# A pair's second 64-row passes on 64 rows of TensorE, two side by side

## The chip, the cores and the metric

The kernel runs on one core of a Trainium2 chip. Times are device microseconds (us) of one execution. The time of the kernel before is the median of three runs. The profile is of one further execution, and every duration below that is not called a run's time is from it. The engines are named as in the profile: PE is TensorE (matmuls), PEld its weight loads, DVE is VectorE, ACT is ScalarE, POOL is GpSimd, SP issues transfers.

## What is computed

One pre-normalised transformer layer on 2048 tokens of width 576, all in 32-bit floats: an attention half (32 heads of 18, each query seeing 8 keys at distances 0, 2, ..., 14), then a gated feed-forward half of width 4608. The change touches only the feed-forward half.

```python
def _B_ref(x, w_gate, w_up, w_down):
    g = jnp.einsum("bsd,df->bsf", x, w_gate)
    u = jnp.einsum("bsd,df->bsf", x, w_up)
    h = _sigmoid(g) * u
    return jnp.einsum("bsf,fd->bsd", h, w_down)

h = x + _A_ref(_layernorm(x, axis=-1), A_wqkv, A_wo)
h2 = h + _B_ref(_layernorm(h, axis=-1), B_w_gate, B_w_up, B_w_down)
```

## The kernel before

**Precision.** A matmul here reads its operands in a shorter float format. To keep 32-bit accuracy every operand is split into a high half and a low half (`split`, L103 to L106: ACT copies to the short format, DVE subtracts to get the rest), and a product is three matmuls: high x high, high x low, low x high. `prod` (L557) does that for two 128-row slices of the inner dimension, so it is six matmuls of 128 rows by 512 tokens.

**The 64-row rest.** The inner dimension is 576 = 4 x 128 + 64. The last 64 rows are held twice, in rows 0 to 63 and again in rows 64 to 127 of one slice. For the activations `split_rest` (L108) puts the high half into all 128 rows and then overwrites rows 64 to 127 with the low half. For the weights both copies are split alike, into a high tile (index 0) and a low tile (index 1). `rest` (L566) then needs two matmuls over 128 rows: with the high weights (a = 0) it gives high x high and high x low at once, and with the low weights (a = 1) it gives low x high, plus low x low.

**Chunks.** The 4608 columns of the feed-forward are worked off in chunks of 128 (NF = 36), for four blocks of 512 tokens, in two halves p = 0 and p = 1. `items` lists them in order: 14 chunks of kind "std" for p = 0 (one block, function `single`), 22 of kind "pair" for p = 0 (two blocks at once), 14 std and then 36 pair for p = 1: 58 pair chunks in all. A pair chunk computes gate and up of two blocks by seven products instead of eight (a scheme of sums and differences of sub-matrices: a00, a01, a11 and s1 to s4 are activations or their sums, t1 to t4 and b00, b10, b11 weights or their sums), and four rests: gate ("g4") and up ("u4") for each of the two blocks.

**A pair chunk** (`pair`, L623) has three accumulators in PSUM, one bank each: b1, b2, b3. Their contents are taken off on the way into s1, s2, s3 in SBUF by ACT copies and DVE additions (L628, L633, L638, L645, L646, L651), and sigmoid is applied to s1 and s2 (L634, L652). `last` multiplies: s1 by what b1 holds at the end, s2 by s3 (L582, or L985 where the results are kept for a seven-product down projection). `between(i)` puts other work between the products: the down projection of earlier chunks (L671 for ordinary ones, L733 for the seven-product kind that the second 36 pair chunks use), and in the first 22 pair chunks attention and output projection of the two later blocks. In those, `between(6)` and `between(4)` issue two units of it, in the last 36 each `between` issues one. A unit of `down_seven` is six matmuls of 288 columns, a unit of the ordinary kind twelve.

**Order.** The program text is not the final order: a scheduler places the instructions of each engine by priorities (`tc.high_priority`) and by the engines' expected load. Every engine then works through its own list strictly in order, and waits at semaphores. A bank is written again only when what it held has been read: the next chunk's first product into b1 waits for DVE's multiplication of s1 by b1, and the product "t4" into b3 waits for the DVE addition of L646.

Of the kernel before, what the change touches and what calls it, by code (L numbers as in the profile page):

```python
# [17 lines left out]
AF = mybir.ActivationFunctionType  # L18
ALU = mybir.AluOpType
# [34 lines left out]
HC = 700  # L54
# [7 lines left out]
def kernel(ctx, tc, x, wqkv, wo, wmlp, out):  # L62
    nc = tc.nc
    dve, act, pool, pe, sp = nc.vector, nc.scalar, nc.gpsimd, nc.tensor, nc.sync
# [34 lines left out]
    def f32(ap):  # L99
        return ap.bitcast(F32)  # L100
# [3 lines left out]
    def split(hi, lo, src):  # L104
        act.activation(hi, src, AF.Copy)  # L105
        splits.append(dve.tensor_tensor(lo, src, f32(hi), ALU.subtract))  # L106

    def split_rest(t, src):  # L108
        act.activation(t, src, AF.Copy)
        dve.tensor_tensor(t[64:128], src[64:128], f32(t[64:128]), ALU.subtract)  # L110

    def pads(g):
        for e in range(2):
# [162 lines left out]
    def th_tile():  # L276
        return xt.tile([P, 5, TB], F32R, tag="th", bufs=3, name="th")

    def tl_tile():
        return xt.tile([P, 4, TB], F32R, tag="tl", bufs=4, name="tl")  # L280

    def x_half(raw, rest):
        t = tl_tile() if rest is None else th_tile()
        split(t[:, 0:2], t[:, 2:4], raw)
        if rest is not None:
            split_rest(t[:, 4], rest)
        return t


    xt = ctx.enter_context(sb_pool("xt"))  # L290
# [53 lines left out]
    def qkv_w(g):  # L344
        w = saw.tile([P, 2, 5, NQ], F32R, tag="qw", bufs=2, name="qw")
        if g == 0:
            wr = swo.tile([P, 5, NQ], F32, tag="wo", name="wr")
        for c in range(5):
            ws = wr[:, c] if g == 0 else sas.tile([P, NQ], F32, tag="wst", bufs=3, name="ws")
            sp.dma_start(ws, wqkv[g][:, c * NQ:(c + 1) * NQ])  # L350
            with tc.high_priority(3 * HI if g == 0 else HI):
                split(w[:, 0, c], w[:, 1, c], ws)
        return w
# [59 lines left out]
    w = [qkv_w(0)]  # L413
# [63 lines left out]
    X = {}  # L477
# [79 lines left out]
    def prod(ps, xx, w, n, first):  # L557
        wt, k0 = w[n]
        k = 0
        for c in range(2):  # L560
            for a, m in ((0, 0), (0, 2), (1, 0)):
                pe.matmul(ps, wt[:, a, k0 + c], xx[:, m + c], start=first and k == 0,  # L562
                          stop=k == 5, skip_group_check=True)
                k += 1

    def rest(ps, xx, w, n):  # L566
        wt, k0 = w[n]
        for a in range(2):
            pe.matmul(ps, wt[:, a, k0], xx[:, 4], start=False, stop=a == 1,  # L569
                      skip_group_check=True)  # L570

    gc_bufs = 3

    def halves(name, src):
# [10 lines left out]
    def s_tile():  # L585
        return gh.tile([P, TB], F32, tag="s", bufs=4, name="s")

    def b_tile(i):
        return gp.tile([P, TB], F32, name=f"b{i % 3 + 1}")
# [31 lines left out]
    added = [None]  # L621

    def pair(X, w, between, last):  # L623
        b1, b2, b3 = b_tile(0), b_tile(1), b_tile(2)
        s1, s2, s3 = s_tile(), s_tile(), s_tile()
        prod(b1, X["a00"], w, "b00", True)
        with tc.high_priority(HC):
            act.activation(s1, b1, AF.Copy)  # L628
        between(0)
        prod(b2, X["a01"], w, "b10", True)  # L630
        rest(b2, X["a01"], w, "g4")
        with tc.high_priority(HC):
            added[0] = dve.tensor_tensor(s1, s1, b2, ALU.add)  # L633
            act.activation(s1, s1, AF.Sigmoid)  # L634
        between(1)
        prod(b1, X["s2"], w, "t2", False)
        with tc.high_priority(HC):
            act.activation(s2, b1, AF.Copy)  # L638
        between(2)
        prod(b3, X["s3"], w, "t3", True)  # L640
        between(3)
        prod(b1, X["s1"], w, "t1", False)
        rest(b1, X["a11"], w, "u4")
        with tc.high_priority(HC):
            act.activation(s3, b1, AF.Copy)  # L645
            added[0] = dve.tensor_tensor(s3, s3, b3, ALU.add)  # L646
        between(4)
        prod(b3, X["a11"], w, "t4", False)
        rest(b3, X["a11"], w, "g4")
        with tc.high_priority(HC):  # L650
            added[0] = dve.tensor_tensor(s2, s2, b3, ALU.add)  # L651
            act.activation(s2, s2, AF.Sigmoid)  # L652
        between(5)
        prod(b1, X["s4"], w, "b11", False)
        rest(b1, X["s4"], w, "u4")
        with tc.high_priority(HC):
            last((s1, b1), (s2, s3))
        between(6)

# [158 lines left out]
    def operands(pp, p, Xn, names, a0, a1):  # L818
        if p == 0:
            a0 = pp.tile([P, 5, TB], F32, name="ar0")  # L820
            pool.dma_start(a0, xscr[0])
        s = [pp.tile([P, 2, TB], F32, name=f"rs{i}") for i in range(3)]
        rd = pp.tile([P, TB], F32, name="rd")
        if p == 1:
            for n in ("a00", "a01"):
                a = a0[:, 0:2] if n == "a00" else a0[:, 2:4]
                with tc.high_priority(HI):
                    Xn[n] = x_half(a, None if n == "a00" else a0[:, 4])
                yield
        raw = yield from sums(a0, a1, a1[:, 0:2] if p == 1 else a0[:, 0:2], *s, rd)  # L830
        for n in names:
            with tc.high_priority(HI):
                Xn[n] = x_half(*raw[n])
            yield
        return raw

# [13 lines left out]
    Xn = {}  # L850
# [33 lines left out]
    raw = None  # L884
# [165 lines left out]
    for c, (kind, p, f) in enumerate(items):  # L1050
        w, d = wc
        for b, late_c in ((0, NF + NSTD - 3), (1, NF + NSTD + 5)):
            if c == late_c:
                e, hf = BLOCKS[b]
                pool.dma_start(ov[e, hf], hacc[b])
        skip = () if kind == "std" else (3,)
        by_seven = c >= NF + NSTD
        if c == NSTD:
            finish_bg()
            last_x = splits[-1]  # L1060
            bg = under_rest(getattr(last_x, "ins", last_x))
        if c == NF + NSTD:
            finish_bg()
            with tc.high_priority(HI):
                for n in ("s1", "a11"):
                    Xn[n] = x_half(*raw[n])
            X = Xn
            pp_stk.close()
            dw = ctx.enter_context(sb_pool("dw", "right"))
        if c + 1 < len(items):  # L1070
            wc = weights(items[c + 1][0], wg, c + 1 < NF + NSTD)
        if c + 2 < len(items):
            wg = load_gu(items[c + 2][2], n=WC if c + 2 < NF + NSTD else GU)
        hid = {}
        blocks = [p] if kind == "std" else [2 * p, 2 * p + 1]

        def last(h0, h1):
            hid[0] = hidden(*h0, "h0")
            hid[1] = hidden(*h1, "h1")

        if kind == "std":
            hid = single(X, w, p, late, twice)
        elif not by_seven:
            side = last_pair if c == NF - 1 else bg_step

            def between(i):
                if i in (4, 6):
                    units(2)
                side(i)

            pair(X, w, between, last)
        else:
            def between(i):
                nonlocal st, gc, gc_bufs, dk
                units(1)
                if c == NF + NSTD and i == 5:
                    assert not queue
                    st_stk.close()
                    gc_stk.close()
                    gc = gc_stk.enter_context(sb_pool("gc2"))  # L1100
                    st = st_stk.enter_context(sb_pool("st2"))
                    dk = dk_stk.enter_context(sb_pool("dk", "right"))
                    for n in ("s4h", "s4l", "s1h"):
                        dk.tile([P, TB], F32R, name=n)
                    gc_bufs = 2
                down_side(f, i)

            pair(X, w, between, last if f >= NF - NPL else last_sums(f))
            if f < NF - NPL:
                if f % 2:  # L1110
                    if f == 1:
                        queue.append(lag(LAG))
                    queue.append(seven())
                continue
            d = M[f]
        seg.append((hid, d))
        if len(seg) == 2:
            if by_seven and f == NF - NPL + 1:
                queue.append(load_tails())
            for b in blocks:  # L1120
                queue.append(down_std(seg, b, f // 2) if kind == "std" else
                             down_tail(seg, b, f == NF - 1) if by_seven else down_units(seg, b))
            seg = []
# [44 lines left out]
```

## Time and profile before

| | |
|---|---|
| time, median of 3 runs | 1635.3 us (1633.71 to 1636.6) |
| span of the profiled execution, first to last instruction | 1628.5 us, 6.8 us under the median of the runs |
| mean granted TensorE clock | 0.987 |
| first pair chunks (22), us from the span's start | about 410 to 799 |
| last pair chunks (36), then the rest of the down projection | 988 to about 1600, to 1628.5 |
| ACT busy | 888.6 us (55%) |
| matmuls in all / in second passes of rests | 8532 / 288 of 576 under L569 |

A busy matmul in the profile includes the time until its last result is out, so that two in a row overlap; the distance of their starts tells the speed. Idle time of PE shorter than that overlap doesn't show as idle.

### The profile page before, as it was taken

How to read it: one execution, taken by the hardware profiler on the slowest of the kernel's cores; microseconds unless marked ns; L12 is line 12 of the kernel's file. 1: busy time of each engine (PE TensorE's matmuls, PEld its weight loads, DVE VectorE, ACT ScalarE, POOL GpSimd, SP SyncE). 2: the span in 40 equal slices, each digit the busy share in tenths (PEclk: the TensorE clock that was granted, in tenths of full speed). 3: DMA queues.
4: the chain of work that ended last, by engine and by line, in shares of the span. 5: the costliest groups of instructions: out<-in, count | busy, mean ns of one | idle time of the engine just before them, and what ended most of it. 6: DMA issues, size and time to landing. Idle time of an engine off the chain costs nothing.

```text
span 1628.5 us, 22454 instructions
## 1 busy us (share of the span) xinstructions
PE 1573.4 (97%) x8532; PEld 1387.9 (85%) x8532; DVE 1265.6 (78%) x1982; ACT 888.6 (55%) x1565; POOL 188.9 (12%) x230
## 2 busy tenths in 40 slices
PE   6799999989999999999989999999999999999998
PEld 6699988778888888888878988888888888888888
DVE  6899898847999999999636677777667777667755
ACT  5423235425556556655534344777667777667761
POOL 2000010010000100100101100112222121211210
PEclk9999999989999999999999999999999999999999
DMA  6545745565665666576685224698888888888883
GB/s 214 184 141 187 264 179 189 156 194 158 194 160 152 168 151 169 160 184 161 171 249 181 100 87 132 141 186 169 177 173 164 184 180 166 181 170 170 189 174 121
DMA packets 77789, 278.23 MB, mean 171 GB/s; under 512 B 8336, under 2 KB 14224, under 8 KB 76784
## 3 DMA queue, kind: packets, MB, share of 16 engines
q0 software_dynamic: 28944, 111.19, 36.1%
q1 hardware_dynamic: 40304, 143.70, 26.7%
q10 hardware_dynamic: 8432, 21.89, 3.5%
q8 instruction: 67, 1.10, 0.3%
q14 instruction: 42, 0.34, 0.1%
HBM read 145.88 MB, written 133.23 MB: 171 GB/s over the span
## 4 chain that ended last, share of the span: by engine, by line
PE 77%; DVE 10%; DMA 8%; issue 2%; ACT 2%; SPq 0%; POOL 0%; ACTq 0%; DVEq 0%; POOLq 0%
PE b L562 39%; PE dp L671 13%; PE dp L733 11%; PE b L569 7%; DMA wg<-in_wmlp_dram 3%; PE acc L151 3%; DVE pr L173 2%; DVE pr L199 2%; DVE lg L176 1%; DMA o<-kw 1%; PE bgp L151 1%; PE b L151 1%; DVE w L106 1%; DMA oj<-o 1%; DMA kw<-k 1%
## 5 line engine op out<-in xcount | busy, mean ns | idle before, releaser
L562 PE MATMUL b<-tl,w 128*128 128x512 f32 x1728 | 446.4, 397 | 3.0 <-ACT w L105 2.1
L562 PEld LDWEIGHTS b<-tl,w 128*128 128x128 f32 x1728 | 313.0, 189 | 64.5 <-ACT w L105 2.9
L562 PE MATMUL b<-th,w 128*128 128x512 f32 x1380 | 362.0, 397 | 4.4 <-DVE s L646 4.3
L562 PEld LDWEIGHTS b<-th,w 128*128 128x128 f32 x1380 | 252.1, 189 | 59.2 <-DVE s L646 9.7
L569 PE MATMUL b<-th,w 128*128 128x512 f32 x576 | 178.1, 390 | 0.0
L105 ACT ACTIVATE w<-wg 128x384 fp32r<-128x384 f32 (+2 forms) x200 | 117.4, 595 | 111.1 <-DMA wg<-in_wmlp_dram 60.1
L106 DVE TENSOR_TENSOR w<-wg,w 128x384 fp32r<-128x384 f32 (+2 forms) x200 | 128.4, 648 | 63.0 <-ACT w L105 59.5
L739 ACT ACTIVATE ev<-dp 128x576 f32<-128x576 f32 x224 | 145.1, 648 | 33.5 <-PE dp L733 30.7
L742 POOL DMA_DIRECT2D h<-ev x128 | 110.6, 864 | 454.7 <-ACT ev L739 438.0
L151 PE MATMUL acc<-qw,th 128*128 128x432 f32 x512 | 156.8, 368 | 4.3 <-ACT th L105 4.3
L106 DVE TENSOR_TENSOR w<-tw,w 128x512 fp32r<-128x512 f32 x116 | 79.6, 687 | 72.2 <-ACT w L105 71.3
L569 PEld LDWEIGHTS b<-th,w 128*128 128x128 f32 x576 | 108.4, 188 | 23.3
L671 PE MATMUL dp<-d,h1h 128*128 128x288 f32 x640 | 120.5, 297 | 6.5 <-ACT stage L679 6.5
L671 PE MATMUL dp<-d,h0h 128*128 128x288 f32 x640 | 119.2, 296 | 3.0 <-ACT h0h L105 2.1
L105 ACT ACTIVATE w<-tw 128x512 fp32r<-128x512 f32 x116 | 73.2, 631 | 89.4 <-PE b L562 84.1
L671 PEld LDWEIGHTS dp<-d,h1h 128*128 128x128 f32 x640 | 99.4, 190 | 9.7 <-ACT stage L679 6.7
L151 PEld LDWEIGHTS acc<-qw,th 128*128 128x128 f32 x512 | 99.5, 194 | 9.5 <-ACT th L105 4.8
L671 PEld LDWEIGHTS dp<-d,h0h 128*128 128x128 f32 x640 | 99.4, 189 | 7.0 <-ACT h0h L105 2.3
L679 ACT ACTIVATE stage<-dp 128x576 f32<-128x576 f32 x112 | 72.0, 645 | 53.9 <-PE dp L671 42.6
L151 PE MATMUL acc<-qw,tl 128*128 128x432 f32 x256 | 94.4, 369 | 0.0
L362 ACT ACTIVATE ev<-acc 128x432 f32<-128x432 f32 x64 | 33.9, 532 | 106.7 <-PE acc L154 96.2
L173 DVE TENSOR_TENSOR pr<-kw,q 128x1152 f32<-128x1152 f32 x64 | 85.0, 1352 | 7.6 <-DMA kw<-k 7.0
(268 smaller groups left out, 2892.7 us busy)
## 6 DMA issues: line engine op xcount, KB each, us to landing
h<-ev POOLq DMA_DIRECT2D x96, 576.0 KB, 6.8
wg<-in_wmlp_dram SPq DMA_DIRECT2D x49, 928.0 KB, 4.9
h<-stage POOLq DMA_DIRECT2D x28, 1152.0 KB, 10.8
wg<-in_wmlp_dram SPq DMA_DIRECT2D x36, 640.0 KB, 4.8
kw<-k SPq DMA_DIRECT2D x16, 792.0 KB, 4.8
vw<-v SPq DMA_DIRECT2D x16, 792.0 KB, 5.5
wd<-in_wmlp_dram SPq DMA_DIRECT2D x18, 576.0 KB, 6.7
h<-ev POOLq DMA_DIRECT2D x32, 288.0 KB, 6.1
```

Source lines behind the costliest of these rows:

```text
L105: act.activation(hi, src, AF.Copy)
L106: splits.append(dve.tensor_tensor(lo, src, f32(hi), ALU.subtract))
L151: pe.matmul(ps[:, :n], a[:, c, js], m[:, c], start=k == 0, stop=False)
L173: dve.tensor_tensor(pr[:, i], kw[:, j:j + W], q[:, j].unsqueeze(1).broadcast_to([P, W, CG]), ALU.mult)
L362: act.activation(ev[:, :, j], ps[:, :NQ].rearrange("p (t c) -> p t c", t=3), AF.Copy)
L562: pe.matmul(ps, wt[:, a, k0 + c], xx[:, m + c], start=first and k == 0, stop=k == 5, skip_group_check=True)
L569: pe.matmul(ps, wt[:, a, k0], xx[:, 4], start=False, stop=a == 1, skip_group_check=True)
L671: pe.matmul(ps[:, i, :DH2], a[:, js], d[:, m, i * DH2:(i + 1) * DH2], start=k == 0, stop=k == n)
L679: act.activation(hv, ps, AF.Copy)
L733: pe.matmul(ps[:, i, :DH2], a[x][:, js], m[y], start=k in (0, 1, 3) and q == 0, stop=q == 2, skip_group_check=True)
L739: act.activation(hs[:, k % 2], ps[:, :, :DH2], AF.Copy)
L742: pool.dma_start(hsev[:, u, k0:k + 1], hs[:, :k + 1 - k0], accum_op=ALU.add, max_dma_last_dim=8 * D)
```

## The change

`rest` stays for std chunks. In a pair chunk it is taken apart. `rest_full` does the pass with the high weights over 128 rows, where the rest was before. The pass with the low weights needs only the 64 rows in which the activation's high half lies; `rest_halves` issues two such passes, of two different rests into two different banks, one in rows 0 to 63 (UP) and one in rows 64 to 127 (DOWN). So that each couple has one of both, the operand a11 now holds its low half in rows 0 to 63 and its high half in rows 64 to 127 (`low_of`), the other way round than a01 and s4. Low x low falls away.

The first couple (b2 with a01 and g4, b1 with a11 and u4) stands behind the product t3, ahead of t1. The second (b3 with a11 and g4, b1 with s4 and u4) stands at the chunk's end. With them DVE's addition and ACT's sigmoid of s1 move behind the first couple, and those of s2 to the chunk's end, ahead of `last`.

```diff
-    def split_rest(t, src):
+    def split_rest(t, src, low=slice(64, 128)):
         act.activation(t, src, AF.Copy)
-        dve.tensor_tensor(t[64:128], src[64:128], f32(t[64:128]), ALU.subtract)
+        dve.tensor_tensor(t[low], src[low], f32(t[low]), ALU.subtract)
...
+    UP, DOWN = slice(0, 64), slice(64, 128)
+
+    def low_of(name):
+        return UP if name == "a11" else DOWN
...
+    def rest_full(ps, xx, w, n):
+        wt, k0 = w[n]
+        pe.matmul(ps, wt[:, 0, k0], xx[:, 4], start=False, stop=True, skip_group_check=True)
+
+    def rest_halves(*outs):
+        for (ps, xx, n, rows), w in outs:
+            wt, k0 = w[n]
+            pe.matmul(ps, wt[rows, 1, k0], xx[rows, 4], start=False, stop=True,
+                      skip_group_check=True)
...
         prod(b2, X["a01"], w, "b10", True)
-        rest(b2, X["a01"], w, "g4")
-        with tc.high_priority(HC):
-            added[0] = dve.tensor_tensor(s1, s1, b2, ALU.add)
-            act.activation(s1, s1, AF.Sigmoid)
+        rest_full(b2, X["a01"], w, "g4")
...
         prod(b3, X["s3"], w, "t3", True)
         between(3)
+        rest_halves(((b2, X["a01"], "g4", UP), w), ((b1, X["a11"], "u4", DOWN), w))
+        with tc.high_priority(HC):
+            added[0] = dve.tensor_tensor(s1, s1, b2, ALU.add)
+            act.activation(s1, s1, AF.Sigmoid)
         prod(b1, X["s1"], w, "t1", False)
-        rest(b1, X["a11"], w, "u4")
+        rest_full(b1, X["a11"], w, "u4")
...
         prod(b3, X["a11"], w, "t4", False)
-        rest(b3, X["a11"], w, "g4")
+        rest_full(b3, X["a11"], w, "g4")
+        between(5)
+        prod(b1, X["s4"], w, "b11", False)
+        rest_full(b1, X["s4"], w, "u4")
+        rest_halves(((b3, X["a11"], "g4", DOWN), w), ((b1, X["s4"], "u4", UP), w))
         with tc.high_priority(HC):
             added[0] = dve.tensor_tensor(s2, s2, b3, ALU.add)
             act.activation(s2, s2, AF.Sigmoid)
-        between(5)
-        prod(b1, X["s4"], w, "b11", False)
-        rest(b1, X["s4"], w, "u4")
-        with tc.high_priority(HC):
             last((s1, b1), (s2, s3))
         between(6)
```

Where the operands are made, `x_half(*raw[n])` becomes `x_half(*raw[n], low_of(n))`.

The order that the scheduler makes of it, at three places of one of the last 36 pair chunks. First PE from the product t3 to the rest of "u4" (b1 to b3 are the accumulators, th and tl activations, w1 to w4 weights, dp an accumulator of the down projection, h0h and h0l its operands). Before:

```order
L562 MATMUL b3_11860<-tl_8823,w2_11651 128x512 x6
L733 MATMUL dp_11919<-d_11691,h0h_11632 128x288
L733 MATMUL dp_11919<-d_11691,h0l_11633 128x288
L733 MATMUL dp_11919<-d_11691,h0h_11632 128x288 x2
L733 MATMUL dp_11919<-d_11691,h0l_11633 128x288
L733 MATMUL dp_11919<-d_11691,h0h_11632 128x288
L562 MATMUL b1_11858<-tl_9155,w3_11652 128x512 x6
L569 MATMUL b1_11858<-th_9158,w4_11650 128x512 x2
```

The same place after the change:

```order
L567 MATMUL b3_11860<-tl_8823,w2_11651 128x512 x6
L749 MATMUL dp_11916<-d_11691,h0h_11632 128x288
L749 MATMUL dp_11916<-d_11691,h0l_11633 128x288
L749 MATMUL dp_11916<-d_11691,h0h_11632 128x288 x2
L749 MATMUL dp_11916<-d_11691,h0l_11633 128x288
L749 MATMUL dp_11916<-d_11691,h0h_11632 128x288
L584 MATMUL b2_11859<-th_8744,w1_11647 128x512
L584 MATMUL b1_11858<-th_9158,w4_11650 128x512
L567 MATMUL b1_11858<-tl_9155,w3_11652 128x512 x6
L579 MATMUL b1_11858<-th_9158,w4_11650 128x512
```

The two rows of L584 are the couple, of 64 rows each (the sizes printed are those of the result); one row of the rest behind t1 is gone. The couple's second half is the first in this chunk to need the low half of the weights w4, and it waits for both DVE and ACT, the wait for one of them being an instruction of its own in PE's queue.

Second, PE at the chunk's end, up to the next chunk's first product into b1. Before:

```order
L562 MATMUL b1_11858<-th_8826,w4_11650 128x512 x5
L569 MATMUL b1_11858<-th_8826,w4_11650 128x512 x2
L733 MATMUL dp_11981<-d_11766,s3h_11823 128x288
L733 MATMUL dp_11981<-d_11766,s3l_11824 128x288
L733 MATMUL dp_11981<-d_11766,s3h_11823 128x288 x2
L733 MATMUL dp_11981<-d_11766,s3l_11824 128x288
L733 MATMUL dp_11981<-d_11766,s3h_11823 128x288
L733 MATMUL dp_11919<-d_11812,s1h_11827 128x288
L733 MATMUL dp_11919<-d_11812,s1l_11828 128x288
L733 MATMUL dp_11919<-d_11812,s1h_11827 128x288 x2
L562 MATMUL b1_12008<-tl_8727,w1_11840 128x512 x6
```

And after the change, from the couple at the chunk's end on:

```order
L584 MATMUL b3_11860<-th_9158,w1_11647 128x512
L584 MATMUL b1_11858<-th_8826,w4_11650 128x512
L749 MATMUL dp_11981<-d_11766,s3h_11823 128x288
L749 MATMUL dp_11981<-d_11766,s3l_11824 128x288
L749 MATMUL dp_11981<-d_11766,s3h_11823 128x288 x2
L749 MATMUL dp_11981<-d_11766,s3l_11824 128x288
L749 MATMUL dp_11981<-d_11766,s3h_11823 128x288
L749 MATMUL dp_11916<-d_11812,s1h_11827 128x288
L749 MATMUL dp_11916<-d_11812,s1l_11828 128x288
L749 MATMUL dp_11916<-d_11812,s1h_11827 128x288 x2
L749 MATMUL dp_11916<-d_11812,s1l_11828 128x288
L749 MATMUL dp_11916<-d_11812,s1h_11827 128x288
```

Behind these stand one matmul of the next chunk's "b10" into b2 and then its first product into b1. Between the old chunk's last matmul and the next one into b1 there were 10 matmuls of 288 columns; now there are 12 and one of 512.

Third, DVE at the same chunk's end (s, r00 and r10 are gate, up and their products; tw and w are the weights of later chunks). Before:

```order
L651 TENSOR_TENSOR s_11862<-s_11862,b3_11860 128x512
L106 TENSOR_TENSOR w3_11845<-tw_11846,w3_11845 128x512
L106 TENSOR_TENSOR w1_11990<-wg_11856,w1_11990 128x640
L985 TENSOR_TENSOR r00_11973<-s_11861,b1_11858 128x512
L985 TENSOR_TENSOR r10_11979<-s_11862,s_11863 128x512
L106 TENSOR_TENSOR w4_11843<-wg_11663,w4_11843 128x384
```

After:

```order
L106 TENSOR_TENSOR w3_11845<-tw_11846,w3_11845 128x512
L548 TENSOR_TENSOR tw_11996<-wg_11856 128x512
L549 TENSOR_TENSOR tw_11996<-wg_11856,tw_11996 128x256
L671 TENSOR_TENSOR s_11862<-s_11862,b3_11860 128x512
L1001 TENSOR_TENSOR r00_11973<-s_11861,b1_11858 128x512
L106 TENSOR_TENSOR w4_11843<-wg_11663,w4_11843 128x384
```

The addition of b3 to s2 (L671, L651 before) now stands right ahead of the multiplication that frees b1 (L1001, L985 before), and both wait for the couple; the weight splits that stood between them have moved ahead or behind.

More of the change, by code (lines that the diff above doesn't have):

```diff
@@ L280, in tl_tile, with x_half @@
         return xt.tile([P, 4, TB], F32R, tag="tl", bufs=4, name="tl")
-    def x_half(raw, rest):
+    def x_half(raw, rest, low=slice(64, 128)):
         t = tl_tile() if rest is None else th_tile()
@@ L285, in x_half @@
         if rest is not None:
-            split_rest(t[:, 4], rest)
+            split_rest(t[:, 4], rest, low)
         return t
+    UP, DOWN = slice(0, 64), slice(64, 128)
+    def low_of(name):
+        return UP if name == "a11" else DOWN
     xt = ctx.enter_context(sb_pool("xt"))
@@ L832, in operands @@
             with tc.high_priority(HI):
-                Xn[n] = x_half(*raw[n])
+                Xn[n] = x_half(*raw[n], low_of(n))
             yield
@@ L1065 @@
                 for n in ("s1", "a11"):
-                    Xn[n] = x_half(*raw[n])
+                    Xn[n] = x_half(*raw[n], low_of(n))
             X = Xn
```

## The prediction

> **What bounds the kernel now.** I read the page's engine totals first, then the chain that ended last, then busy time by stage, then PE's rows in order of time.
>
> ```profile
> PE 1573.4 (97%) x8532; PEld 1387.9 (85%) x8532; DVE 1265.6 (78%) x1982; ACT 888.6 (55%) x1565; POOL 188.9 (12%) x230
> PE 77%; DVE 10%; DMA 8%; issue 2%; ACT 2%; SPq 0%; POOL 0%; ACTq 0%; DVEq 0%; POOLq 0%
> PE b L562 39%; PE dp L671 13%; PE dp L733 11%; PE b L569 7%; DMA wg<-in_wmlp_dram 3%; PE acc L151 3%; DVE pr L173 2%; DVE pr L199 2%; DVE lg L176 1%; DMA o<-kw 1%; PE bgp L151 1%; PE b L151 1%; DVE w L106 1%; DMA oj<-o 1%; DMA kw<-k 1%
> ...
> L569 PE MATMUL b<-th,w 128*128 128x512 f32 x576 | 178.1, 390 | 0.0
> ```
>
> PE is busy 97% of the span and 77% of the chain runs through it; the rests (L569) alone are 7% of the chain. DVE and DMA have their share of the chain mostly in the attention, ahead of the pair chunks. In the stages where the change acts:
>
> ```profile
> 410.00:799.00 389.00, 385.65 (x2108) 339.25 (x2107) 371.31 (x502) 224.97 (x368) 29.96 (x28) 1.00 0.63 165
> 988.00:1628.50 640.50, 634.39 (x3386) 548.27 (x3384) 454.62 (x770) 422.65 (x736) 112.55 (x130) 1.00 0.81 169
> ```
>
> The columns are length, then busy time of PE, PEld, DVE, ACT and POOL, granted clock, DMA share, GB/s. The first row is the 22 pair chunks of p = 0: PE is idle 3.4 us of 389, so a matmul saved there is time saved, but DVE is busy 371.3 of 389 (95%) as well. The second is the 36 pair chunks of p = 1 and the tail: PE idle 6.1 us of 640.5, DVE 71%. The granted clock is 1.00 in both, so there is no clock to win or lose at the level seen.
>
> **What a rest costs.** Duration is not the price, since matmuls overlap. In order of time:
>
> ```profile
> 701.09 0.62 PE L569 MATMUL b<-th,w 128*128 128x512 f32 x2
> 701.54 1.52 PE L562 MATMUL b<-th,w 128*128 128x512 f32 x6
> 702.90 0.62 PE L569 MATMUL b<-th,w 128*128 128x512 f32 x2
> 703.36 0.42 PE L671 MATMUL dp<-d,h0h 128*128 128x288 f32 x2
> ```
>
> Six matmuls start within 702.90 - 701.54 = 1.36 us, 0.227 us each, and a rest's two take 0.46 us. One lasts 0.390 us (the L569 row), so the last 0.163 us of each lie beneath the next one.
>
> **Removed:** four second passes in each of 58 chunks, 4 x 58 x 0.227 = 52.7 us of PE. **Added:** two couples of 64-row matmuls in each chunk, 116 couples. No row of this trace has a matmul over fewer than 128 rows, so a couple's price is bounded. From below: both stream at once and it takes one place, 0.227 us; saving 116 x 0.227 = 26.3 us. From above, without a cost at its borders: the halves follow each other, 0.454 us; saving nothing. Between them stands how far ahead a second weight load can go.
>
> ```profile
> 700.87 0.41 PEld L569 LDWEIGHTS b<-th,w 128*128 128x128 f32 x2
> 701.32 0.41 PEld L562 LDWEIGHTS b<-th,w 128*128 128x128 f32 x2
> 79.23 0.66 PE L140 MATMUL mm<-ident,tok 128*128 128x128 f32 x4 [1.52 <-ACT tok L132]
> ```
>
> The first two rows begin one matmul ahead: the rest's loads begin at 700.87 while its matmuls begin at 701.09, and the loads of the next product at 701.32, 0.23 after 701.09, with the rest's second matmul. One load is made ahead, and the next begins when that matmul has begun. The third row shows what a load needs where matmuls are too short to hide it: four transposes of 128 columns in 0.66 us, each lasting 0.273 in the median of its group, so (0.66 - 0.273) / 3 = 0.129 us from start to start with a load for each.
>
> ```profile
> L140 PE MATMUL mm<-ident,tok x80: 270/273/476, 9.1 to 221.8; 128*128 128x128 f32 x80
> ```
>
> If the second half's load begins only with the first half's matmul, the second half starts 0.129 us behind the first, and the couple takes 0.227 + 0.129 = 0.356 us. I take this value, since every load in the rows behaves so; it saves 0.454 - 0.356 = 0.098 us per couple, 116 x 0.098 = **11.4 us** (4.3 in the first stage, 7.1 in the second).
>
> The Trainium skill, "TensorE: Matmul & The Clock Gate", section "Part 3: Packing small matmuls — row/col tiling", says that matmuls in different row groups start about 4 ns apart and that a load overlaps a running matmul when its row group differs. By it a couple would be an estimated 0.231 us and the saving 25.9 us; no run here shows it yet, and its bound is in the range already.
>
> **What moves, and its cover.** (1) The addition and sigmoid of s1 go behind the first couple. s1 is needed by `last` at the chunk's end, some 7 us of PE work later: nothing. (2) The couple needs the copy of b1 to s2 done; t1, which stood at that place, needed the same: nothing. The low half of w4 is needed eight matmuls earlier (1.8 us), but it is split near the chunk's start:
>
> ```profile
> 1381.34 1.64 PE L562 MATMUL b<-tl,w 128*128 128x512 f32 x6
> ...
> 1381.77 0.55 DVE L106 TENSOR_TENSOR w<-wg,w 128x384 fp32r<-128x384 f32 x1
> ```
>
> That is 0.4 us into a chunk in which the couple stands about 7 us in: nothing. The couple's extra wait is an instruction of its own in PE's queue:
>
> ```profile
> L562 PEldq EVENT_SEMAPHORE  x8: 51/51/51, 254.5 to 982.1; - x8
> ```
>
> It takes 0.051 us; PE's queue runs a load ahead of the matmuls, so 0.227 us of a running matmul hide it: nothing, and without that cover 58 x 0.051 = 3.0 us. (3) The chunk's end is the tight place:
>
> ```profile
> 1377.97 0.61 PE L569 MATMUL b<-th,w 128*128 128x512 f32 x2
> 1378.62 0.69 DVE L651 TENSOR_TENSOR s<-s,b 128x512 f32<-128x512 f32 x1 [0.83 <-PE b L569]
> 1379.23 0.69 DVE L106 TENSOR_TENSOR w<-tw,w 128x512 fp32r<-128x512 f32 x1
> 1379.56 0.61 PE L569 MATMUL b<-th,w 128*128 128x512 f32 x2
> 1379.83 0.82 DVE L106 TENSOR_TENSOR w<-wg,w 128x640 fp32r<-128x640 f32 x1
> 1380.01 0.30 PE L733 MATMUL dp<-d,s3h 128*128 128x288 f32 x1
> 1380.57 0.68 DVE L985 TENSOR_TENSOR r<-s,b 128x512 f32<-128x512 f32 x1
> 1380.80 0.30 PE L733 MATMUL dp<-d,s1h 128*128 128x288 f32 x1
> ```
>
> Before, b3's addition (L651) ran beneath the product of s4. The rest of b1 ended at 1379.56 + 0.61 = 1380.17; DVE could have multiplied at 1380.21 (it starts 0.04 after a matmul, as L651 did at 1378.58), but was in a split until 1380.57, 0.36 late. It ended at 1381.25, and PE began the next product into b1 at 1381.34 (the row above), so this place has no slack. After the change DVE must first add b3 (0.61 from start to start, 1378.62 to 1379.23), then multiply: 0.04 + 0.61 + 0.68 + 0.09 = 1.42 us from the couple's end to the next b1. The cover is 12 matmuls of 288 columns at (1380.80 - 1380.01) / 6 = 0.132 us, 1.58 us, which begin 0.163 us ahead of that end: 1.42 us. The cover holds exactly when DVE is free. If DVE is late as above, 0.36 us in each of 36 chunks give back 13 us; never late, nothing. The order has put no split between addition and multiplication, so I take 0.05 us a chunk, **1.8 us**. In the first stage two ordinary units, 24 matmuls or 3.2 us, stand there: nothing. The last chunk's s2 is 1.3 us later, beneath the first block's tail of the down projection.
>
> **Sum.** -11.4 + 1.8 = -9.6 us: a span of 1628.5 - 9.6 = 1618.9, and with the 6.8 us by which the median of the runs lies over the profiled span, **1625.7 us**. With the bounds of the couple's price, 26.3 saved less 1.8 gives 1610.8, and with a late DVE and a couple at 0.356 it is 1637.
>
> **Rivals.** *A border costs the overlap (slower).* Every matmul in the trace starts 0.163 us before the one ahead has ended, but all use the same 128 rows. If one of another row height starts only when the array is empty, each couple pays that tail when it begins and again when the 128-row work resumes: 2 x 0.163 = 0.326 us, against a saving of 0.098. 116 x 0.228 = +26.4 us, with the 1.8 1663; with halves at once 116 x (0.326 - 0.227) = +11.5, 1648.6. It decides from 0.049 us per border on (0.113 with halves at once). For it: PE's rows hold nothing but 128-row work, so none speaks against it. Against it: the 0.163 us is the way through the array and out of it, and rows that are free from the start need not wait for all of it.
>
> The Trainium skill, "TensorEngine Tiling (Array Packing)", section "Key Properties", states outright that changing the tiling mode drains TensorE while tiles within a mode run independently. By that rule the change goes the way of this rival; the trace before can neither confirm nor refute it.
>
> *No overlap (same).* The two halves are issued as two ordinary matmuls, one behind the other: 116 x 0 saved, 1.8 lost, 1637. For it: the array may take only one stream at a time, and the trace never shows two. The change then does not do what it says.
>
> *DVE takes the place of PE.* DVE is 95% busy in the first pair stage. It has the same operations after the change; with 4.3 us less it would be 371.3 of 384.7 (97%), with 10 us less 98%. If it can't, the first stage's 4.3 are lost and the chunk's end in the second stage pays 13 instead of 1.8: 1635.3 - 11.4 + 4.3 + 13 = 1641. I count half of this case to the same, half to the slower.
>
> **How the numbers follow.** The forecast (halves overlap at least in part, borders free) 0.48, own range 1611 to 1632. Borders cost the tail 0.32, no overlap 0.14, DVE 0.06. A measurement of this kernel can tell about 0.2%, 3.3 us, from no change. Faster: 0.47, the forecast less a little that lands within 3.3 us. Same: no overlap, half the DVE case, and borders near 0.05 us, 0.20. Slower: the rest, 0.33. The range reaches from 1610 to 1656: it takes in both ends of the forecast and the slower rival up to about three quarters of its price.
>
> **What would show it.** The couple's two matmuls: right if they start less than 0.227 us apart with the next 128-row matmul about 0.23 after the second; 0.13 apart by my value, near 0 by the lower bound, 0.23 for no overlap. Borders: the start distances into and out of a couple, 0.227 if free, about 0.39 if the array empties. DVE: the wait of the next chunk's first product into b1 for the multiplication, near 0.05 us a chunk against 0.36. Chunks of the first stage should shorten by 0.2 us. I am wrong if 128-row matmuls beside a couple slow down or the chunk's end waits for DVE in most chunks.

## The result, and the profile after

| | before | after |
|---|---|---|
| median of four runs | 1635.95 us | 1653.01 us |
| span of the profiled execution | 1628.5 us | 1649.8 us |
| mean granted TensorE clock | 0.987 | 0.987 |

The four runs of before are the three behind the 1635.3 us above and one more. One of the four runs after took 5347.41 us; the ratio below goes by the other three (1650.06 to 1653.97 us, median 1652.04).

The kernel after takes 1.0097 times as long, with a 95% interval of 1.0075 to 1.0118: it is slower, by about 16 us in the runs and by 21.3 us between the two profiled executions. The profile's page after, with the engine totals and the chain that ended last by engine and by line:

```profile
PE 1592.7 (97%) x8532; PEld 1362.8 (83%) x8532; DVE 1268.7 (77%) x1982; ACT 885.9 (54%) x1565; POOL 188.7 (11%) x230
...
PE 49%; issue 25%; DVE 10%; DMA 8%; POOL 5%; ACT 2%; SPq 0%; POOLq 0%; ACTq 0%; DVEq 0%
PE b L567 23%; PE dp L687 8%; PE dp L749 6%; PE acc L151 4%; DMA wg<-in_wmlp_dram 4%; POOL h L758 3%; PE b L579 2%; PE b L584 2%; DVE pr L173 2%; DVE pr L199 1%; DVE lg L176 1%; PE bgp L151 1%; DMA o<-kw 1%; PE b L151 1%; POOL h L703 1%
```

PE has as many matmuls as before and 232 of them over half the rows, yet it is busy 19.3 us longer (1592.7 against 1573.4). No other engine took the time: DVE's total rose by 3.1 us, ACT's fell by 2.7. In the chain PE lost 28 points, and "issue" won 23, time in which the engine waited for nothing that the profile shows. Its size isn't the loss (25% of the span is 412 us), but its kind is a hint: what PE lost has no releaser. By stage (columns as in the prediction):

```profile
410.00:800.00 390.00, 387.07 (x2063) 321.89 (x2062) 367.57 (x496) 221.21 (x362) 29.95 (x28) 1.00 0.62 162
...
990.00:1649.00 659.00, 651.75 (x3418) 539.70 (x3417) 458.22 (x772) 423.08 (x739) 112.42 (x130) 1.00 0.81 165
```

In the first row 45 matmuls fewer are done in a stretch that is 1 us longer than the one before (2063 in 390 us, 2108 in 389), at a granted clock of 1.00 and with PE idle for 2.9 us only. So PE itself works more slowly; it doesn't wait for another engine more than it did. From the start of the first pair chunk to the end of that stage it is 397.2 us against 389.4, +7.8 for 22 chunks; the starts of the last 36 chunks span 611.4 us against 599.3, +12.1 for 35. Both are 0.35 us per chunk. The groups of the taken-apart rests (line, engine, operation, tile, shape, count, then busy time and mean ns of one, then idle time ahead and its releasers):

```profile
L579 PE MATMUL b<-th,w 128*128 128x512 f32 x232 | 90.4, 390 | 0.0
L584 PE MATMUL b<-th,w 64*128 64x512 f32 x232 | 59.7, 495 | 1.9 <-ACT s L650 1.9
...
L584 PEld LDWEIGHTS b<-th,w 64*128 64x128 f32 x232 | 22.3, 183 | 37.6 <-issue 35.1 <-ACT s L650 2.5
```

A 64-row pass lasts 495 ns, a 128-row one 390. Busy time counts overlapped work once, so 232 passes of 0.495 us in 59.7 us busy (0.257 each) say that they lie side by side. Ahead of the weight loads of L584, PEld (weight loads) was idle for 37.6 us, 35.1 of it with no releaser. In order of time, PE around a couple of the first stage:

```profile
703.20 2.88 PE L567 MATMUL b<-tl,w 128*128 128x512 f32 x12
706.01 0.50 PE L584 MATMUL b<-th,w 64*128 64x512 f32 x2
706.44 1.66 PE L567 MATMUL b<-tl,w 128*128 128x512 f32 x6
707.94 0.39 PE L579 MATMUL b<-th,w 128*128 128x512 f32 x1
```

The twelve end at 703.20 + 2.88 = 706.08, so the last of them started at 706.08 - 0.39 = 705.69. The couple starts 0.32 us later instead of 0.227, both halves within 0.50 us, so within 0.01 of each other. The next 128-row matmul starts 0.43 after them. The six of 706.44 take 1.50 us to the start of the rest at 707.94, where six take 1.36 elsewhere: the first of them is long. The chunk's end shows the same with the weight loads (the number in brackets is idle time ahead and its releaser):

```profile
1396.18 0.39 PE L579 MATMUL b<-th,w 128*128 128x512 f32 x1
1396.50 0.19 PEld L584 LDWEIGHTS b<-th,w 64*128 64x128 f32 x2 [0.35 <-issue]
1396.50 0.49 PE L584 MATMUL b<-th,w 64*128 64x512 f32 x2
...
1396.93 0.19 PEld L749 LDWEIGHTS dp<-d,s3h 128*128 128x128 f32 x1 [0.24 <-issue]
1396.93 0.40 PE L749 MATMUL dp<-d,s3h 128*128 128x288 f32 x1
...
1397.03 0.19 PEld L749 LDWEIGHTS dp<-d,s3l 128*128 128x128 f32 x1
1397.16 0.29 PE L749 MATMUL dp<-d,s3l 128*128 128x288 f32 x1
1397.17 0.32 PEld L749 LDWEIGHTS dp<-d,s3h 128*128 128x128 f32 x2
1397.26 0.68 DVE L671 TENSOR_TENSOR s<-s,b 128x512 f32<-128x512 f32 x1
...
1397.85 0.68 DVE L1001 TENSOR_TENSOR r<-s,b 128x512 f32<-128x512 f32 x1
...
1398.62 0.40 PE L567 MATMUL b<-th,w 128*128 128x512 f32 x1
...
1398.86 0.39 PE L567 MATMUL b<-tl,w 128*128 128x512 f32 x1
```

At each of the two borders, into the couple and out of it, the load starts within 0.01 us of its matmul, at 1396.50 and at 1396.93, not one matmul ahead as in an unbroken stream of 128-row matmuls; and the first matmul behind the border is longer by what shows of that load, 0.49 instead of 0.39 and 0.40 instead of 0.29. The load of 1397.03 is 0.13 us ahead of its matmul again.

Over all couples of the trace, the medians of the start distances are: last 128-row matmul to the first half 0.318 us, one half to the other 0.003, halves to the next 128-row matmul 0.428, from that to its successor 0.338 where both have 512 columns. Against 0.227 the way in is 0.091 longer, the block itself 0.201, the way out 0.106 (288 columns) to 0.111. I read it as two equal borders of 0.20 us: 0.091 in which nothing starts, and about 0.109 of weight load that is not hidden, which falls to the matmul behind the border. A couple with its borders then takes 0.091 + 0.428 + 0.109 = 0.63 us in place of two passes, 0.454: 0.174 dearer, 0.35 for the two of a chunk, as the stages show. Summed over the trace (four couples have another matmul between their halves, and pay four borders instead of two) the blocks take 77.2 us in place of the 52.7 removed, +24.5. All other waits of PE, the start distances beyond the ordinary one, are 84.4 us against 87.9: -3.5. Together +21.0, against +21.3 of the spans.

### The profile page after: what moved, and what is told of

Its sections match the earlier page's. It is cut to its first block, busy times and chain, and to the rows that moved or that the text cites. A ratio compares the mean times of both kernels' runs of the same rounds, so it can differ in the third digit from the quotient of the medians.

```text
span 1649.8 us, 22486 instructions
## 1 busy us (share of the span) xinstructions
PE 1592.7 (97%) x8532; PEld 1362.8 (83%) x8532; DVE 1268.7 (77%) x1982; ACT 885.9 (54%) x1565; POOL 188.7 (11%) x230
## 4 chain that ended last, share of the span: by engine, by line
PE 49%; issue 25%; DVE 10%; DMA 8%; POOL 5%; ACT 2%; SPq 0%; POOLq 0%; ACTq 0%; DVEq 0%
PE b L567 23%; PE dp L687 8%; PE dp L749 6%; PE acc L151 4%; DMA wg<-in_wmlp_dram 4%; POOL h L758 3%; PE b L579 2%; PE b L584 2%; DVE pr L173 2%; DVE pr L199 1%; DVE lg L176 1%; PE bgp L151 1%; DMA o<-kw 1%; PE b L151 1%; POOL h L703 1%
## 5 line engine op out<-in xcount | busy, mean ns | idle before, releaser
L567 PE MATMUL b<-tl,w 128*128 128x512 f32 x1728 | 452.3, 399 | 3.3 <-ACT w L105 3.3
L567 PE MATMUL b<-th,w 128*128 128x512 f32 x1380 | 363.9, 397 | 5.0 <-ACT s L661 2.9
L567 PEld LDWEIGHTS b<-th,w 128*128 128x128 f32 x1380 | 254.1, 189 | 59.9 <-ACT s L661 3.8
L105 ACT ACTIVATE w<-wg 128x384 fp32r<-128x384 f32 (+2 forms) x200 | 112.7, 596 | 173.4 <-PE b L584 76.2
L106 DVE TENSOR_TENSOR w<-wg,w 128x640 fp32r<-128x640 f32 (+2 forms) x200 | 126.9, 649 | 57.7 <-ACT w L105 55.4
L579 PE MATMUL b<-th,w 128*128 128x512 f32 x232 | 90.4, 390 | 0.0
L703 POOL DMA_DIRECT2D h<-stage x28 | 33.6, 1199 | 476.6 <-ACT stage L695 333.5
```

The costliest lines, as they stand in the source:

```text
L579: pe.matmul(ps, wt[:, 0, k0], xx[:, 4], start=False, stop=True, skip_group_check=True)
L703: pool.dma_start(hacc[b], hs, accum_op=ALU.add, max_dma_last_dim=8 * D)
```

## The experiments

The theory after this reading was that **each change of row height costs** 0.20 us, whatever the order and however many 64-row matmuls stand between two changes. Its rivals: that the new **order** costs the time (waits for DVE or ACT at the moved places), that **64-row matmuls** are slow in themselves, and that the **halves** don't overlap after all. Each time stands beside runs of the kernel before on the same chip.

**1. The new order with 128 rows.** From the kernel after:

```diff
-            pe.matmul(ps, wt[rows, 1, k0], xx[rows, 4], start=False, stop=True,
+            pe.matmul(ps, wt[:, 1, k0], xx[:, 4], start=False, stop=True,
```

> The order of the changed kernel with its second passes over all 128 rows (low x low is added again). Border theory (what costs is the change between 128-row and 64-row work, 0.40 us a couple: 0.09 for the array to empty and 0.11 for a weight load not made ahead, at each of two borders, against 0.227 saved): the loss goes altogether, and since all other waits of PE in the changed kernel's trace sum to 3.5 us less than before, 1632 to 1636 us. Order theory (the loss is the additions and sigmoids moved to the chunk's end): 1650 or more.

Measured: 1636.35 us, ratio 1.0014 (0.9995 to 1.0032). The chunk's end, PE in order of time:

```profile
1382.03 0.39 PE L579 MATMUL b<-th,w 128*128 128x512 f32 x1
1382.26 0.61 PE L584 MATMUL b<-th,w 128*128 128x512 f32 x2
1382.71 0.30 PE L749 MATMUL dp<-d,s3h 128*128 128x288 f32 x1
1382.85 0.30 PE L749 MATMUL dp<-d,s3l 128*128 128x288 f32 x1
```

At the same place over all rows the distances are 0.23, 0.45 for the two, 0.14, and no matmul is long. The moved sigmoids, the extra wait and the chunk's end cost nothing that can be measured (the interval allows -0.8 to +5 us); the loss is in the 64-row passes. The order theory falls as the cause of the loss. The trace of this run has about 5.7 us more of PE's other waits than the kernel before, in which the order may have a part; the kernel after, in the same order, has 3.5 us less.

**2. Four single 64-row passes in a chunk, in the order of before.** From the kernel before, in `pair` alone:

```diff
+    def rest_single(ps, xx, w, n):
+        wt, k0 = w[n]
+        pe.matmul(ps, wt[:, 0, k0], xx[:, 4], start=False, stop=False, skip_group_check=True)
+        pe.matmul(ps, wt[0:64, 1, k0], xx[0:64, 4], start=False, stop=True,
+                  skip_group_check=True)
...
-        rest(b2, X["a01"], w, "g4")
+        rest_single(b2, X["a01"], w, "g4")
```

(The three other rests are changed alike. No second half stands beside the 64-row pass, it is in rows 0 to 63 alone, and it goes on in the bank of the matmul ahead of it.)

> The order of before, each second pass of a pair's rests alone on 64 rows, not coupled: 232 blocks of one 64-row matmul. Border theory: nothing is saved and 232 x 0.40 = +93 us, about 1729 us; starts 0.32 us into, 0.43 out of each block. Theory that two matmuls side by side disturb each other: no loss here, about 1636. Order theory: 1636.

Measured, in two runs: 1714.21 us, ratio 1.0489 (1.0454 to 1.0525), +79 us. The chunk's end:

```profile
1392.16 0.40 PE L574 MATMUL b<-th,w 128*128 128x512 f32 x1
1392.48 0.50 PE L575 MATMUL b<-th,w 64*128 64x512 f32 x1
1392.91 0.40 PE L739 MATMUL dp<-d,s3h 128*128 128x288 f32 x1
1393.15 0.29 PE L739 MATMUL dp<-d,s3l 128*128 128x288 f32 x1
```

One 64-row pass costs what a couple costs: 0.32 in, 0.43 for the block, 0.24 out instead of 0.13. So it is not the two halves that disturb each other, nor the change of bank inside a couple. With twice as many borders as in the kernel after the loss is four times as large or more, since nothing is saved in return: 232 x 0.40 = 93. In the trace the 232 blocks take 145.9 us in place of 52.7, +93.2 as expected, and the other waits of PE 6.7 us less; the profiled span is 86.5 longer. The runs show 14 us less than the 93: part of it is that a slower PE waits less for others, the rest lies between the profiled execution and the median.

**3. Each couple twice between the same borders.** From the kernel after:

```diff
-        for (ps, xx, n, rows), w in outs:
+        for (ps, xx, n, rows), w in outs + outs:
```

> Each couple is issued twice in a row, so each second pass is added twice. Border theory: the second couple has no border and takes one place of 0.227 us, 116 x 0.227 = +26 us over the changed kernel, 1679 us. If the cost is one of every couple (0.40 + 0.227 each time): +73 us, 1726 us. If the second couple only overlaps in part, by a load made late, 0.356 each: +41 us, 1694 us.

Measured: 1678.91 us, ratio 1.0272 (1.025 to 1.0294), some 27 us more than the kernel after.

```profile
1395.86 0.39 PE L579 MATMUL b<-th,w 128*128 128x512 f32 x1
1396.17 0.73 PE L584 MATMUL b<-th,w 64*128 64x512 f32 x4
1396.84 0.40 PE L749 MATMUL dp<-d,s3h 128*128 128x288 f32 x1
1397.08 0.29 PE L749 MATMUL dp<-d,s3l 128*128 128x288 f32 x1
```

Four halves take 0.67 us to the next 128-row matmul (median 0.662), 0.234 more than two. The medians inside a block also part the border: the second couple starts 0.332 us behind the first (0.227 and 0.105 for the first couple's late load), its own loads are ahead again by 0.23 us, and the next 128-row matmul starts 0.324 us behind it (0.227 and 0.097). So a second couple costs one place of 0.227 and no border: 64-row matmuls are not slow in themselves, the change of height is.

**4. Both halves in the same rows.** From the kernel after:

```diff
-        return UP if name == "a11" else DOWN
+        return DOWN
...
-        rest_halves(((b2, X["a01"], "g4", UP), w), ((b1, X["a11"], "u4", DOWN), w))
+        rest_halves(((b2, X["a01"], "g4", UP), w), ((b1, X["a11"], "u4", UP), w))
...
-        rest_halves(((b3, X["a11"], "g4", DOWN), w), ((b1, X["s4"], "u4", UP), w))
+        rest_halves(((b3, X["a11"], "g4", UP), w), ((b1, X["s4"], "u4", UP), w))
```

> The couples as in the changed kernel, but both halves in rows 0 to 63, so that they cannot run side by side. If overlap is real and worth one place: +26 us over the changed kernel, 1679 us, with the second half starting about 0.23 us after the first. If the records 0.003 us apart are only how such matmuls are recorded and they run one after the other anyway: no change, 1653 us.

Measured: 1677.83 us, ratio 1.026 (1.0234 to 1.0286), some 26 us more than the kernel after.

```profile
1393.50 0.39 PE L579 MATMUL b<-th,w 128*128 128x512 f32 x1
1393.82 0.73 PE L584 MATMUL b<-th,w 64*128 64x512 f32 x2
1394.48 0.40 PE L749 MATMUL dp<-d,s3h 128*128 128x288 f32 x1
```

Two halves in one half of the array take the time of four in both: the second starts 0.335 us behind the first, where 0.23 was expected. The 0.108 beyond 0.227 belong to the load of the first half, which stands behind the border and lasts 0.493 us; the load of the second starts 0.228 us ahead of its matmul, which lasts 0.393 us, and is hidden though it is for the same rows. The borders are as before. The overlap of the kernel after is real, and worth one place for each couple.

**5. One couple in a chunk instead of two.** From the kernel after, the first couple back to passes over 128 rows:

```diff
+    def rest_low(ps, xx, w, n):
+        wt, k0 = w[n]
+        pe.matmul(ps, wt[:, 1, k0], xx[:, 4], start=False, stop=True, skip_group_check=True)
...
-        rest_halves(((b2, X["a01"], "g4", UP), w), ((b1, X["a11"], "u4", DOWN), w))
+        rest_low(b2, X["a01"], w, "g4")
+        rest_low(b1, X["a11"], w, "u4")
```

> The changed kernel with its first couple made over 128 rows again, one pass behind the other; the couple at the chunk's end stays on 64 rows. Border theory: 58 of 116 couples are left, 58 x (0.40 - 0.227) = +10 us over the kernel before, 1645 us. If the loss sits in one place, at the chunk's end (the moved addition of b3 ahead of the multiplication that frees b1) or at the first couple with its second wait: all of it, 1652 us, or none, 1635 us.

Measured: 1642.42 us, ratio 1.0047 (1.0031 to 1.0063), +8.2 us, half of what the kernel after loses. The 58 couples that are left show 0.091 in, 0.424 for the block, 0.106 out: the loss goes with the number of borders.

**6. Both couples of a chunk as one block.** If four halves stand between two borders, a block takes about 0.86 us in place of 0.908 for four passes. From the kernel before: the four second passes are put in one block behind the product t4, in the last 36 pair chunks. b1 is not finished with s4 there, so "u4" of a11 needs a bank of its own, b4, which DVE adds to s3. `rest_high` is the pass with the high weights, `rest_low` the one with the low weights over 128 rows, and `rest_block` issues the 64-row passes listed in it. In the first 22 pair chunks b4 is None. From `pair`, at the product t4:

```diff
...
-        rest(b3, X["a11"], w, "g4")
+        high = rest_high(b3, X["a11"], w, "g4")
+        if b4 is None:
+            rest_low(b3, X["a11"], w, "g4")
+        else:
+            with tc.issue_after(getattr(high, "ins", high)):
+                rest_block(w, (b2, X["a01"], "g4", UP), (b4, X["a11"], "u4", DOWN),
+                           (b1, X["s4"], "u4", UP), (b3, X["a11"], "g4", DOWN), own=b4)
         with tc.high_priority(HC):
+            if b4 is not None:
+                dve.tensor_tensor(s1, s1, b2, ALU.add)
+                act.activation(s1, s1, AF.Sigmoid)
             added[0] = dve.tensor_tensor(s2, s2, b3, ALU.add)
             act.activation(s2, s2, AF.Sigmoid)
+            if b4 is not None:
+                dve.tensor_tensor(s3, s3, b4, ALU.add)
...
```

> In the last 36 pair chunks all four second passes stand in one block of two couples, behind t4's rest; a11 with u4 goes to a bank of its own (free there), which DVE adds to s3. The first 22 pair chunks are as before. Border theory: a block costs 0.40 + 2 x 0.227 = 0.855 us in place of 4 x 0.227 = 0.908, 36 x -0.053 = -2 us against before, about 1633 us, level with before as near as can be measured. If each couple pays on its own: 36 x 2 x 0.173 = +12 us, 1647 us. If the added DVE operation (0.69 us a chunk) shows: up to +25 us more.

Measured: 1644.35 us, ratio 1.0058 (1.0045 to 1.0072), +10 us. The expectation of 1633 us was missed. The time is near the 1647 us of the rival "each couple pays on its own", but the block's rows are against it:

```profile
1405.84 0.39 PE L579 MATMUL b<-th,w 128*128 128x512 f32 x1
1406.16 0.49 PE L589 MATMUL b<-th,w 64*128 64x512 f32 x1
1406.16 0.49 PE L589 MATMUL bgp<-th,w 64*128 64x512 f32 x1
1406.50 0.40 PE L589 MATMUL b<-th,w 64*128 64x512 f32 x2
1406.82 0.40 PE L770 MATMUL dp<-d,s2h 128*128 128x288 f32 x1
```

The block takes 0.66 us, with its borders 0.86, and the 36 together 31.5 us in place of 32.7. But PE's other waits are 102.9 us against 87.9 before. DVE at a chunk's end:

```profile
1389.65 0.69 DVE L682 TENSOR_TENSOR s<-s,b 128x512 f32<-128x512 f32 x1 [0.72 <-PE bgp L589]
1390.26 0.68 DVE L687 TENSOR_TENSOR s<-s,bgp 128x512 f32<-128x512 f32 x1
1390.86 0.68 DVE L684 TENSOR_TENSOR s<-s,b 128x512 f32<-128x512 f32 x1
1391.45 0.69 DVE L106 TENSOR_TENSOR w<-tw,w 128x512 fp32r<-128x512 f32 x1
1392.06 0.68 DVE L1022 TENSOR_TENSOR r<-s,b 128x512 f32<-128x512 f32 x1
```

The three additions and a split stand back to back ahead of the multiplication, which ends at 1392.74. On PE:

```profile
1392.57 0.29 PE L770 MATMUL dp<-d,s1l 128*128 128x288 f32 x1
1392.79 1.65 PE L567 MATMUL b<-tl,w 128*128 128x512 f32 x6
```

The next product into b1 starts at 1392.79, 0.05 behind the multiplication and 0.22 behind the matmul ahead of it, where 0.13 would do. 32 chunk ends lose 0.10 us so, some 3 of the 15. Two other waits in the last stage's rows make some 7 more. At the stage's start PE waits for DVE's addition of b3 to s3 (L670) until 1009.43, 4.04 us, and until 1024.52, 0.92 us, where before the longest such wait is 1.21 us; and in 15 chunks PE waits for ACT to take a result of the down projection out of its bank, 0.11 us and 0.10 more for the load behind the wait, 3 us in all. Some 3.6 us lie ahead of this stage, where this kernel has the passes of before. That the extra addition makes DVE late is argued from these rows, not tried by itself.

**7. 128-row passes twice.** Experiment 1 with `outs + outs`, the counterpart of experiment 3: the same products, without borders.

```diff
-        for (ps, xx, n, rows), w in outs:
+        for (ps, xx, n, rows), w in outs + outs:
...
-            pe.matmul(ps, wt[rows, 1, k0], xx[rows, 4], start=False, stop=True,
+            pe.matmul(ps, wt[:, 1, k0], xx[:, 4], start=False, stop=True,
```

> The counterpart of the kernel with every couple twice: the same order, each second pass twice, but over 128 rows, four in a row. Border theory: 232 more matmuls of 0.227 us, 1636 + 53 = 1689 us; the kernel with two couples to a block took 1679, and a block of two couples should cost 0.855 us in place of 0.908, 116 x 0.053 = 6 us less. If two couples to a block still lose against 128 rows, this kernel is faster than 1679 us.

Measured: 1678.28 us, ratio 1.027 (1.024 to 1.0301), +45 us and level with experiment 3 (1.0272), 11 us under the 1689 us expected. By the start distances 116 blocks of 0.86 us should be 5 us cheaper than 116 of 0.908, but experiment 3 doesn't have 116: four of its couples have other matmuls between their halves and pay more borders, and with them its blocks take 104.9 us in the trace against 105.3 for the 128-row passes. So no difference was to be expected between these two kernels, and none is seen. As in experiment 2 the added 52.7 us of PE work bring less than that, with PE's other waits 5.7 us below those of before. Two couples between two borders neither won nor lost measurably here.

No kernel here beats the one before. The most that the start distances promise, one block of four in each of 58 chunks without anything else getting worse, is 58 x (0.908 - 0.862) = 2.7 us, less than can be measured.

## Why the prediction was wrong

The forecast was 1625.7 us, faster; it is 1653.0, slower. The time lies in the range only because the range takes in three quarters of the first rival's price; the sign is wrong. **The step that failed** is the one that set the forecast apart from that rival: "borders free", a term put at nothing. No row spoke for it, since the trace before had 128-row matmuls only, and the one reason given against the rival, that rows free from the start need not wait for all of the tail, leaves open how much they wait. A border costs 0.20 us, so that a couple pays 0.40 us for the 0.227 it saves.

- *The couple's price.* I took 0.356 us, the second half 0.129 behind the first because "every load in the rows behaves so". The halves start 0.003 apart, as the load of one half does not wait for the other's matmul; the lower bound of 0.227 was right (a second couple in the same block adds 0.234), and experiment 4 shows what halves in the same rows cost. The sum was thus too low in its saving, 11.4 us instead of about 26, and had that been all, the kernel would have been faster by more than forecast. The 0.129 was misread, too: of the four transposes of 79.23 the second starts 0.165 us behind the first and the others 0.109, which is also the median of all transposes in a row in that trace. So the price of a load that nothing hides, the larger part of a border, stood in the trace before.
- *The rival "a border costs the overlap"* named the mechanism, and in its form "with halves at once" also the state that came. Its size was off: it priced a border at the tail of 0.163 us and gave +11.5. Its tail measures 0.091: the couple starts about 0.07 us before the recorded end of the matmul ahead, so part of the tail still overlaps. What it lacked altogether is the weight load, 0.109 per border, which is not made ahead across a change of height. 2 x 0.20 - 0.227 = 0.17 per couple is +20 for 116 couples, and the trace has +24.5 with the split ones. It was to decide from 0.113 us per border on, and 0.20 is well beyond that.
- *The chunk's end.* I took 1.8 us given back because DVE would be late now and then. In the rows from 1397.26 DVE adds b3 and multiplies back to back, ends at 1398.53, and the next product into b1 starts at 1398.86, right behind the matmul of 1398.62: PE doesn't wait. In the whole trace after, no wait of PE is put down to this multiplication (L1001). The cover was counted too short: the order shows one matmul of 512 columns behind the 12, another 0.227 us, which hide that DVE starts its addition 0.27 us behind the couple's end instead of 0.04.
- *The moved sigmoids, the low half of w4, the extra wait.* Costed at nothing; experiment 1 with the same order measures 1.0014 (0.9995 to 1.0032). The wait is there (0.051 us, 55 times) and hidden: the first couple of a chunk, which nearly always has it, starts 0.088 us late in the median, the one at the chunk's end 0.091.

```profile
L584 PEldq EVENT_SEMAPHORE  x55: 51/51/51, 414.9 to 1610.2; - x55
```

- *"No overlap"* falls by experiment 4, which is that case and 26 us dearer. *"DVE takes the place of PE"* falls by the first stage: DVE is busy 367.6 of 390 us there, less than the 371.3 of 389 before, and the stage got slower on PE.

The prediction had cited a sentence on each half of the result. The Trainium skill, “TensorE: Matmul & The Clock Gate”, section “Part 3: Packing small matmuls — row/col tiling”, puts matmuls of different row groups about 4 ns apart; the trace agrees with 3 ns. The Trainium skill, “TensorEngine Tiling (Array Packing)”, section “Key Properties”, says that a change of tiling mode drains TensorE; the trace agrees in part, with 0.091 us during which nothing starts, though the couple starts before the recorded end of the matmul ahead, and such ends are modelled. Neither sentence names the load that is no longer made ahead, the larger part of a border; that was measured here.

What stays open: why nothing starts for 0.091 us, and why a load isn't made ahead across a border; only the times are shown. That a border is the same in both directions is read from the medians by giving each late load to the border ahead of it, as the blocks of experiment 3 bear out; it was not tried by itself. The order alone may still be worth up to some 5 us. Blocks of three couples and more were not tried.

## What to carry to other kernels

Half-height matmuls side by side really do share one place, but each stretch of them pays two changes of height, here 0.40 us, before it saves 0.227 us per couple: count the couples between two changes, not the couples in all. One loses 0.17 us, two come out about even (0.86 us in place of 0.908, and no difference in the runs), and only from three on could it pay (3 x 0.234 + 0.39 = 1.10 us in place of 1.36, an estimate). And a cost for which the trace holds no row is not thereby zero: where a change brings a first of its kind (a new shape between old ones), take the price of entering and leaving it as the largest unknown, and let that set the sign of the forecast.

## What the runs showed of the hardware

- Weight loads that run one matmul ahead in an unbroken stream of 128-row matmuls are not made ahead across a change of row height, in either direction. Their 0.109 us then shows in the duration of the matmul behind the border (0.495 instead of 0.390 us over 512 columns).
- Two 64-row matmuls in different halves of the array start 0.003 us apart, loads included. In the same half the second starts 0.335 us behind the first, of which 0.108 are the first one's late load; the load of the second is hidden.
- PE's busy time rose by 19.3 us while half the rows of 232 matmuls were left out: neither its busy share (97% in both) nor its idle time shows the loss, the start distances do.
